# Interleaved columns in a two-layer FFN: ScalarE and VectorE write the activations in token order, instead of TensorE weaving them a second time

## The chip, the cores and the metric

The kernel runs on one core of a Trainium2 chip. The metric is the time of one execution on the device, in microseconds, as the median of several runs. The profile shows one further execution, in which every instruction's start and length were recorded.

## What is computed

The input x holds 4 sequences of 12480 tokens with 128 channels. An attention through 32 learned vectors mixes each sequence, and a feed-forward layer follows:

```python
def mab(q, kv):
    s = scale * (q @ kv.transpose(0, 2, 1))
    s = s - s.max(-1, keepdims=True)
    a = np.exp(s)
    a /= a.sum(-1, keepdims=True) + 1e-09
    return a @ kv
h = mab(I, x)                    # 32 x 128 per sequence
attn = mab(x, h)                 # 12480 x 128 per sequence
h = attn @ w_in                  # 49920 x 2048
g = np.maximum(0.01 * h, h)
return (g @ w_out).astype(np.float32)
```

## The kernel before

The leaky rectifier is split in two: max(0.01 h, h) = 0.01 h + 0.99 max(h, 0). The part with 0.01 is linear, so it needs one product per tile (the linear product, with the matrix m2s). The other part is the feed-forward layer proper. Since attn is a product of attention weights with the 32 x 128 matrix h, the first layer multiplies the attention weights of a tile by h @ w_in, which is prepared once per sequence (hws).

All products of the feed-forward layer use a 32-bit type that TensorE rounds to fewer bits. To keep the precision, values stand as a rounded part and a rest: A4 holds both parts of a tile's attention weights, ghi and glo those of the activations, w_hi and w_lo those of w_out.

The tokens are worked in tiles of 512 (96 of them, and two smaller pair tiles of 384 that take the ends of two sequences). For each tile there are 16 steps, one per block of 128 of the 2048 hidden units; 98 x 16 = 1568 steps in all. A step u is:

- ffn_first: TensorE multiplies A4 by a block of hws into the PSUM tile ph (L821; 3 buffers). ScalarE writes ghi = Relu(ph), rounded (L829). VectorE writes glo = max(ph, 0) - ghi (L831).
- ffn_second: TensorE adds three products to the PSUM tile po of the tile: ghi by w_hi, glo by w_hi, ghi by w_lo (L849). At the last step of a tile the linear product of A4 and m2s is added (L855), and the tile goes to a store: VectorE transposes po in blocks of 32 x 32 into osb (L865), and four DMAs on the SP queue write it to the output (L883).

The order of all instructions is written out in one loop over u: ffn_first of step u + 3, then ffn_second of step u, then one piece each of the work for the coming tiles and the next sequence (first_scores, first_values, second, stack and so on), with a counter, debt, that spaces the pieces that load VectorE.

**Weaving.** A full tile's columns are its 512 tokens in an order that the loads set; call it the tile's order. woven(x, t) is a view that reads or writes the columns of a tile in the order 0, 256, 1, 257, 2, 258 and so on: two streams, 256 floats (1 KB) apart, taken in turn. TensorE reads A4 through it, so the columns of ph, and then of ghi and glo, stand in woven order. It reads ghi and glo through it again, so the columns of po are woven twice. The linear product must match them, so it reads A4 woven twice, as four streams of 128 columns: 0, 128, 256, 384, 1 and so on. The store's DMAs undo this in the rows that they write. Pair tiles are not woven.

Of the kernel before, what the change touches and what calls it, by code (L numbers as in the profile page):

```python
# [9 lines left out]
F32 = mybir.dt.float32  # L10
# [3 lines left out]
AF = mybir.ActivationFunctionType  # L14
# [5 lines left out]
def induced_attention_then_leaky_ffn(  # L20
# [20 lines left out]
    nc = tc.nc  # L41
# [57 lines left out]
    def gen_ps(name):  # L99
        return ps_h.tile([P, TOK], F32, tag="ph", name=name)  # L100
# [14 lines left out]
    xT, xr, ex, aT, A4, hw, maxima, sums_of = {}, {}, {}, {}, {}, {}, {}, {}  # L115
# [668 lines left out]
    tiles = []  # L784
# [8 lines left out]
    def spans(t):  # L793

        got, at = [], 0
        for b, g, js in tiles[t]:
            n = len(js) * 32 * GROUPS[g][2]
            got.append((b, at, n))
            at += n
        return got, at  # L800

    def woven(tile_, t, times=1):

        if len(tiles[t]) > 1:
            return tile_
        if times == 2:
            return tile_.rearrange("p (a b n) -> p n a b", a=2, b=2)
        return tile_.rearrange("p (a n) -> p n a", a=2)

    live, accs = {}, {}  # L810
    slots = [
# [4 lines left out]
    def ffn_first(u):  # L816
        t, f = slots[u]
        parts, n = spans(t)
        ph = gen_ps("ph")
        for b, o, w in parts:  # L820
            nc.tensor.matmul(  # L821
                ph[:, o : o + w],
                hw[b][1][:, f * P : (f + 1) * P],
                woven(A4[t][:, o : o + w], t),
                start=True,
                stop=True,
            )
        ghi = sb.tile([P, TOK], F32R, tag="ghi", name="ghi", bufs=LOOK + 2)
        nc.scalar.activation(ghi[:, :n], ph[:, :n], AF.Relu)  # L829
        glo = sb.tile([P, TOK], F32R, tag="glo", name="glo", bufs=LOOK + 2)  # L830
        nc.vector.scalar_tensor_tensor(  # L831
            out=glo[:, :n],
            in0=ph[:, :n],
            scalar=0.0,
            in1=ghi[:, :n].bitcast(F32),
            op0=ALU.max,
            op1=ALU.subtract,
        )
        live[u] = (ghi, glo)

    def ffn_second(u):
        t, f = slots[u]
        parts, n = spans(t)
        ghi, glo = live.pop(u)
        if f == 0:
            accs[t] = ps_o.tile([P, TOK], F32, tag="po", name="po")
        po = accs[t]
        for w, r in ((w_hi, ghi), (w_hi, glo), (w_lo, ghi)):
            nc.tensor.matmul(  # L849
                po[:, :n], w[:, f, :], woven(r[:, :n], t), start=(f == 0 and r is ghi and w is w_hi), stop=False  # L850
            )
        if f == NF - 1:
            a4 = A4.pop(t)
            for b, o, w in parts:
                nc.tensor.matmul(  # L855
                    po[:, o : o + w], hw[b][2], woven(a4[:, o : o + w], t, 2),
                    start=False, stop=(o + w == n),
                )

    def store(t):  # L860
        _, n = spans(t)
        po = accs.pop(t)
        yield
        osb = sb.tile([P, TOK], F32, tag="osb", name="osb", bufs=3)
        nc.vector.transpose(osb[:, :n], po[:, :n])  # L865
        yield HEAVY
        o = 0
        for b, g, js in tiles[t]:
            base, J, K = GROUPS[g]
            n = 32 * K  # L870
            for j in js:
                row = b * N + base + j * 32 * K
                if len(tiles[t]) > 1:
                    dst = out[row : row + n, :].rearrange("(r k) c -> r k c", k=K)
                else:
                    dst = out[row : row + n, :].rearrange("(v r u) c -> r u v c", v=4, u=K // 4)
                for cb in range(NB):
                    src = osb[32 * cb : 32 * cb + 32, o : o + n]
                    if len(tiles[t]) > 1:
                        src = src.rearrange("p (k c) -> p k c", c=32)  # L880
                    else:
                        src = src.rearrange("p (u v c) -> p u v c", v=4, c=32)
                    nc.sync.dma_start(dst[..., 32 * cb : 32 * cb + 32], src)  # L883
                o += n
            yield
# [39 lines left out]
    with tc.manual_schedule():  # L925
# [9 lines left out]
        for lane in (  # L935
            one, weights, two, one, weights, one, two, weights, one, one, one, two,
        ):
            step(lane)
        ffn_first(0)
        ffn_first(1)  # L940
        step(two)
        step(two)
        step(turning)
        ffn_first(2)
        step(two)
        stacks[0] = stacks[0][QUICK:]
# [6 lines left out]
        for u in range(NT * NF):  # L953
            t, f = slots[u]
            if f == 0 and tiles[t][0][1:] == (0, [0]):
                b = tiles[t][0][0]
# [3 lines left out]
            if u + LOOK < NT * NF:  # L960
                ffn_first(u + LOOK)
            ffn_second(u)
            if f == NF - 1:
                stores.append(store(t))
# [57 lines left out]
```

## Time and profile before

| | |
|---|---|
| median of 3 runs | 1544.82 us (1544.58 to 1544.96) |
| profiled execution | 1544.46 us |
| its span, first to last instruction | 1542.5 us |
| TensorE (PE) busy | 1516.9 us, 98% |
| VectorE (DVE) busy | 1275.1 us, 83% |
| ScalarE (ACT) busy | 1005.4 us, 65% |
| mean granted TensorE clock | 0.992 |

The profile gives for each engine the time in which it had an instruction under way. PE is TensorE's matmuls, PEld its weight loads, which overlap with them. Matmuls overlap each other too, and the recorded length of one contains its passage through the array: matmuls of 380 ns start 216 ns apart. In the rows quoted, L821 is a line of the kernel; "glo<-ph,ghi" names what is written and read; then come partitions x elements; "x1536" counts the instructions; "busy us, mean ns" follow, then the idle time of the engine just ahead of them and what ended it. A row of waits reads: who waited for whom, microseconds in total, how often, longest. SPq is the DMA queue of SP.

### The profile page before, as it was taken

To read this page: it belongs to the slowest core of one execution; us is meant where nothing else is said; L and a number is where in the kernel's file an instruction comes from. 1 tells how busy PE (TensorE), PEld (TensorE's weight loads), DVE (VectorE), ACT (ScalarE), POOL (GpSimd) and SP (SyncE) were. 2 spreads that over 40 slices of the span, in tenths; PEclk is the share of its full clock that TensorE was granted. 3 is DMA by queue.
4 is the path that set the end of the run, shared out by engine and by line. 5 is a ranking of instruction groups with operands and counts; after the bars stand their busy time and mean duration, and the time that the engine had idled before them with its cause. 6 is when DMAs were issued, how large, how long until landed. Compare 5 with 4: busy or idle time off the path is not lost.

```text
span 1542.5 us, 22596 instructions
## 1 busy us (share of the span) xinstructions
PE 1516.9 (98%) x7965; PEld 1271.0 (82%) x7965; DVE 1275.1 (83%) x2245; ACT 1005.4 (65%) x1770; POOL 99.0 (6%) x100
## 2 busy tenths in 40 slices
PE   7799999999999999999999999999999999999998
PEld 5578888888888888888888888888888898888887
DVE  6678889888888888887888888887888888888886
ACT  6356666666666666666666666666666666666665
POOL 2110010000101000000011000000111000000000
PEclk9799999999999999999999999999999999999999
DMA  8133323452243254541314246432302112112211
GB/s 276 17 78 62 69 44 80 98 110 63 60 89 61 36 97 100 99 93 29 72 41 91 49 77 132 95 74 50 76 16 52 24 37 49 35 35 41 43 27 21
DMA packets 401313, 104.21 MB, mean 68 GB/s; under 512 B 372368, under 2 KB 374832, under 8 KB 401200
## 3 DMA queue, kind: packets, MB, share of 16 engines
q1 hardware_dynamic: 401152, 102.75, 32.3%
q8 instruction: 63, 1.03, 0.3%
q14 instruction: 50, 0.41, 0.1%
q10 hardware_dynamic: 48, 0.02, 0.0%
HBM read 48.94 MB, written 25.56 MB: 48 GB/s over the span
## 4 chain that ended last, share of the span: by engine, by line
PE 96%; DVE 2%; ACT 1%; DMA 0%; issue 0%; SPq 0%; DVEq 0%
PE po L849 65%; PE ph L821 23%; PE s_ps L305 3%; PE po L855 2%; PE h_ps L425 1%; DMA xr<-in_x_dram 0%; DVE glo L831 0%; PE xT_ps L538 0%; DVE cv_a L136 0%; ACT ghi L829 0%; PE a_ps L770 0%; ACT xT L544 0%; DVE cv_t L144 0%; PE q_ps L745 0%; DVE ay L453 0%
## 5 line engine op out<-in xcount | busy, mean ns | idle before, releaser
L829 ACT ACTIVATE ghi<-ph 128x512 fp32r<-128x512 f32 (+1 forms) x1568 | 929.4, 595 | 497.2 <-PE ph L821 492.9
L831 DVE SCALAR_TENSOR_TENSOR glo<-ph,ghi 128x512 fp32r<-128x512 f32 (+1 forms) x1568 | 1034.4, 678 | 234.9 <-ACT ghi L829 210.4
L821 PE MATMUL ph<-A,hws 128*128 128x512 f32 (+1 forms) x1600 | 607.6, 383 | 5.1 <-DVE hws L603 2.8
L849 PE MATMUL po<-ghi,w_hi 128*128 128x512 f32 (+1 forms) x1568 | 595.4, 380 | 2.1 <-DVE osb L865 2.1
L849 PE MATMUL po<-glo,w_hi 128*128 128x512 f32 (+1 forms) x1568 | 594.3, 379 | 0.0
L849 PE MATMUL po<-ghi,w_lo 128*128 128x512 f32 (+1 forms) x1568 | 594.3, 379 | 0.0
L821 PEld LDWEIGHTS ph<-A,hws 128*128 128x128 f32 x1600 | 302.7, 190 | 75.3 <-DVE glo L831 21.5
L849 PEld LDWEIGHTS po<-ghi,w_hi 128*128 128x128 f32 x1568 | 297.6, 190 | 46.1 <-issue 3.3
L849 PEld LDWEIGHTS po<-glo,w_hi 128*128 128x128 f32 x1568 | 297.3, 190 | 41.0
L849 PEld LDWEIGHTS po<-ghi,w_lo 128*128 128x128 f32 x1568 | 297.1, 190 | 41.1
L720 POOL TENSOR_TENSOR alo<-aT,ahi 128x512 fp32r<-128x512 f32 x24 | 30.7, 1278 | 683.6 <-ACT ahi L715 681.1
L865 DVE STREAM_TRANSPOSE osb<-po 128x512 f32<-128x512 f32 (+1 forms) x98 | 68.9, 703 | 1.5 <-PE po L855 1.5
L675 POOL TENSOR_TENSOR y<-y,mx 128x512 f32<-128x512 f32 (+1 forms) x27 | 25.3, 937 | 413.8 <-DVE mx L673 413.8
L406 DVE STREAM_TRANSPOSE xT<-xc 128x512 f32<-128x512 f32 x72 | 50.4, 700 | 0.0
L855 PE MATMUL po<-A,m2s 128*128 128x512 f32 (+1 forms) x100 | 43.2, 436 | 0.0
L689 POOL TENSOR_TENSOR y<-y,sm 128x512 f32<-128x512 f32 (+1 forms) x27 | 25.3, 937 | 183.3 <-DVE sm L687 144.7
L425 PEld LDWEIGHTS h_ps<-xr,ay 128*32 128x32 f32 (+1 forms) x784 | 22.0, 110 | 14.3 <-issue 14.3
L425 PE MATMUL h_ps<-xr,ay 128*32 128x128 f32 (+1 forms) x784 | 27.5, 274 | 1.8 <-DVE ay L453 1.8
L305 PE MATMUL s_ps<-xT,indT 128*32 128x512 f32 x192 | 26.3, 621 | 1.3 <-ACT xT L544 1.3
L305 PE MATMUL s_ps<-xT,hT 128*32 128x512 f32 x192 | 25.6, 605 | 0.0
L317 DVE TENSOR_SCALAR_CACHE_REDUCE e<-s_ps 128x512 f32<-128x512 f32 (+1 forms) x28 | 17.1, 610 | 8.7 <-PE s_ps L305 8.5
L855 PEld LDWEIGHTS po<-A,m2s 128*128 128x128 f32 x100 | 18.9, 189 | 2.5
(111 smaller groups left out, 399.3 us busy)
## 6 DMA issues: line engine op xcount, KB each, us to landing
xr<-in_x_dram SPq DMA_DIRECT2D x96, 256.0 KB, 4.5
out_dram<-osb SPq DMA_DIRECT2D x384, 64.0 KB, 2.2
xc<-in_x_dram SPq DMA_DIRECT2D x288, 64.0 KB, 2.7
A<-ahi SPq DMA_DIRECT2D x188, 64.0 KB, 2.0
A<-alo SPq DMA_DIRECT2D x188, 64.0 KB, 2.0
raw<-in_moe_w_in_dram SPq DMA_DIRECT2D x4, 512.0 KB, 6.7
raw<-in_moe_w_out_dram SPq DMA_DIRECT2D x4, 512.0 KB, 7.4
hws<-hwhi SPq DMA_DIRECT2D x24, 64.0 KB, 2.0
```

What stands on the lines that cost most here:

```text
L305: nc.tensor.matmul(dst, lhsT, rhs, start=True, stop=True)
L406: nc.vector.transpose(t[:, j, :], blk.rearrange("p n c -> p (n c)"))
L425: nc.tensor.matmul(hp[32 * k : 32 * k + 32, :C], ay[:rows, 4 * q + k, :], xb[:rows, k, :], start=(q == 0), stop=(4 * q + 4 >= K), tile_pos ...
L675: eng.tensor_tensor(out=yv, in0=yv, in1=mx[:rows, :K].unsqueeze(2).broadcast_to([rows, K, M]), op=ALU.subtract,)
L689: eng.tensor_tensor(out=yv, in0=yv, in1=smv.unsqueeze(2).broadcast_to([rows, K, M]), op=ALU.mult)
L720: (eng or nc.gpsimd).tensor_tensor(out=alo[sl], in0=aT.pop((b, g))[: 32 * J, :], in1=ahi[sl].bitcast(F32), op=ALU.subtract,)
L821: nc.tensor.matmul(ph[:, o : o + w], hw[b][1][:, f * P : (f + 1) * P], woven(A4[t][:, o : o + w], t), start=True, stop=True,)
L829: nc.scalar.activation(ghi[:, :n], ph[:, :n], AF.Relu)
L831: nc.vector.scalar_tensor_tensor(out=glo[:, :n], in0=ph[:, :n], scalar=0.0, in1=ghi[:, :n].bitcast(F32), op0=ALU.max, op1=ALU.subtract,)
L849: nc.tensor.matmul(po[:, :n], w[:, f, :], woven(r[:, :n], t), start=(f == 0 and r is ghi and w is w_hi), stop=False)
L855: nc.tensor.matmul(po[:, o : o + w], hw[b][2], woven(a4[:, o : o + w], t, 2), start=False, stop=(o + w == n),)
L865: nc.vector.transpose(osb[:, :n], po[:, :n])
```

## The change

ScalarE now writes ghi through woven, and reads ph in pairs of neighbours (paired: the same order as before, split in 256 x 2). So column 0 of ph goes to column 0 of ghi, column 1 to column 256, column 2 to column 1: ghi is back in the tile's order. VectorE does the same with glo, and reads ghi, its second input, through woven. The three products of L849 read ghi and glo through woven, as before, and so po is now woven once. The linear product therefore reads A4 woven once, like L821, and each store writes its rows in two halves of 256 instead of four quarters of 128.

```diff
-    def woven(tile_, t, times=1):
+    def woven(tile_, t):
         if len(tiles[t]) > 1:
             return tile_
-        if times == 2:
-            return tile_.rearrange("p (a b n) -> p n a b", a=2, b=2)
         return tile_.rearrange("p (a n) -> p n a", a=2)
+
+    def paired(tile_, t):
+        if len(tiles[t]) > 1:
+            return tile_
+        return tile_.rearrange("p (n a) -> p n a", a=2)
...
-        nc.scalar.activation(ghi[:, :n], ph[:, :n], AF.Relu)
+        nc.scalar.activation(woven(ghi[:, :n], t), paired(ph[:, :n], t), AF.Relu)
...
         nc.vector.scalar_tensor_tensor(
-            out=glo[:, :n],
-            in0=ph[:, :n],
+            out=woven(glo[:, :n], t),
+            in0=paired(ph[:, :n], t),
             scalar=0.0,
-            in1=ghi[:, :n].bitcast(F32),
+            in1=woven(ghi[:, :n].bitcast(F32), t),
...
                 nc.tensor.matmul(
-                    po[:, o : o + w], hw[b][2], woven(a4[:, o : o + w], t, 2),
+                    po[:, o : o + w], hw[b][2], woven(a4[:, o : o + w], t),
...
-                    dst = out[row : row + n, :].rearrange("(v r u) c -> r u v c", v=4, u=K // 4)
+                    dst = out[row : row + n, :].rearrange("(v r u) c -> r u v c", v=2, u=K // 2)
...
-                        src = src.rearrange("p (u v c) -> p u v c", v=4, c=32)
+                        src = src.rearrange("p (u v c) -> p u v c", v=2, c=32)
```

No instruction changes its place on any engine, and none is added or taken away. What changes is the shape of the evacuations and of the stores. The lines below the views move down by four, so L821, L829, L831, L849, L855 and L865 become L825, L833, L835, L853, L859 and L869. On VectorE, in the middle of the program (xT is the transposed input of the next sequence, e its scores), before:

```order
330 L865 STREAM_TRANSPOSE osb<-po 128x512
331 L831 SCALAR_TENSOR_TENSOR glo<-ph,ghi 128x512 x3
332 L406 STREAM_TRANSPOSE xT<-xc 128x512
333 L831 SCALAR_TENSOR_TENSOR glo<-ph,ghi 128x512 x3
334 L406 STREAM_TRANSPOSE xT<-xc 128x512
```

The same place after the change:

```order
330 L869 STREAM_TRANSPOSE osb<-po 128x512
331 L835 SCALAR_TENSOR_TENSOR glo<-ph,ghi 128x256x2 x3
332 L406 STREAM_TRANSPOSE xT<-xc 128x512
333 L835 SCALAR_TENSOR_TENSOR glo<-ph,ghi 128x256x2 x3
334 L406 STREAM_TRANSPOSE xT<-xc 128x512
```

Nothing moved: between two transposes VectorE still has three evacuations, whose 512 elements are now 256 pairs.

## The prediction

> **What bounds the kernel now.** I read the page first: the shares of the engines and the chain that ended last.
>
> ```profile
> span 1542.5 us, 22596 instructions
> PE 1516.9 (98%) x7965; PEld 1271.0 (82%) x7965; DVE 1275.1 (83%) x2245; ACT 1005.4 (65%) x1770; POOL 99.0 (6%) x100
> PE 96%; DVE 2%; ACT 1%; DMA 0%; issue 0%; SPq 0%; DVEq 0%
> ```
>
> The chain is TensorE from end to end: 96% of the span. VectorE is off the chain, but busy 83% of the time, so it is the engine with the least room. Next, the waits and a few stretches of 20 to 100 us (columns: length, then busy time of PE, PEld, DVE, ACT and POOL with counts, granted clock, DMA).
>
> ```profile
> ACT ghi L829 <- PE ph L821: 492.9, 1431, 3.2
> DVE glo L831 <- ACT ghi L829: 210.4, 593, 2.5
> PEld ph L821 <- DVE glo L831: 21.5, 48, 0.8
> ...
> 0.00:60.00 60.00, 46.08 (x475) 33.79 (x476) 37.16 (x120) 31.02 (x67) 11.59 (x14) 0.86 0.60 188
> 60.00:80.00 20.00, 16.52 (x80) 12.74 (x79) 13.53 (x21) 9.32 (x19) 3.79 (x3) 0.91 0.05 7
> 460.00:560.00 100.00, 100.00 (x507) 84.44 (x506) 87.54 (x162) 66.93 (x120) 9.86 (x9) 1.00 0.31 58
> 1360.00:1460.00 100.00, 100.00 (x463) 87.24 (x462) 81.47 (x121) 68.69 (x116) 2.56 (x2) 1.00 0.17 32
> ```
>
> ScalarE waits for TensorE, VectorE for ScalarE, and TensorE for VectorE in only 48 places, 21.5 us in all. From about 80 us on TensorE is never idle, with VectorE 81 to 88% busy beside it. So a nanosecond saved on TensorE in that stretch is a nanosecond of the span, and VectorE can be slowed until its own work fills the span, not further.
>
> **The linear product.** Here are the matmuls by shape and three in a row at a tile's end (start, length).
>
> ```profile
> L821 PE MATMUL ph<-A,hws 128*128 128x512 f32 x1536 | 596.0, 388 | 5.1 <-DVE hws L603 2.8 <-DVE A L778 2.3
> L849 PE MATMUL po<-ghi,w_hi 128*128 128x512 f32 x1536 | 584.0, 380 | 2.1 <-DVE osb L865 2.1
> L855 PE MATMUL po<-A,m2s 128*128 128x512 f32 x96 | 42.5, 443 | 0.0
> ...
> 305.00 0.44 PE L855 MATMUL po<-A,m2s 128*128 128x512 f32 x1
> 305.27 0.38 PE L821 MATMUL ph<-A,hws 128*128 128x512 f32 x1
> 305.49 0.38 PE L849 MATMUL po<-ghi,w_hi 128*128 128x512 f32 x1
> ```
>
> L821 reads A4 woven once (two column streams, 1 KB apart), L849 reads ghi and glo in the same way, L855 reads A4 woven twice (four streams). The first two take 388 and 380 ns, the third 443. The next matmul starts 0.27 us behind L855 and 0.22 us behind L821. After the change L855 reads exactly as L821 does, so it loses 55 to 63 ns; I take 60. On 96 tiles that is 5.8 us (5.3 to 6.0), all on the chain. The three products of L849 keep their reading pattern and gain nothing. The four pair tiles (32 of 1568 steps) are untouched.
>
> **The two evacuations.** Each of 1536 ScalarE instructions now writes ghi in alternation to two halves 1 KB apart, and each of 1536 VectorE instructions reads ghi and writes glo that way. Reading ph in pairs is still reading it in order: nothing.
>
> ```profile
> L829 ACT ACTIVATE ghi<-ph 128x512 fp32r<-128x512 f32 x1536 | 913.7, 597 | 488.0 <-PE ph L821 483.7
> L831 DVE SCALAR_TENSOR_TENSOR glo<-ph,ghi 128x512 fp32r<-128x512 f32 x1536 | 1017.8, 681 | 232.2 <-ACT ghi L829 207.7
> L831 DVE SCALAR_TENSOR_TENSOR glo<-ph,ghi 128x384 fp32r<-128x384 f32 x32 | 16.8, 543 | 2.8 <-ACT ghi L829 2.6
> ...
> L158 DVE TENSOR_REDUCE e<-ident 128x32 f32<-128x128 f32 x1 | 0.4, 369 | 1.3 <-POOL ident masks.py:199 1.3
> L163 DVE TENSOR_REDUCE own<-ident 128x4 f32<-128x128 f32 x1 | 0.3, 278 | 0.0
> L673 DVE TENSOR_REDUCE mx<-y 128x16 f32<-128x512 f32 x24 | 16.2, 675 | 0.0
> ```
>
> Contiguous, VectorE needs (681 - 543) / 128 = 1.08 ns an element at L831. No row of the trace shows a write that jumps at every element. The nearest is a VectorE read that does: L158 reduces 128 elements of the identity with 128 bytes between neighbours, L163 the same 128 in order. They take 369 and 278 ns, 0.71 ns an element apart; L673 and L163 give 1.03 ns an element for reading in order. So one jumping stream costs VectorE 0.71 x 512 = 364 ns per instruction, if two alternating halves are to it what those four streams were. Bounds: 0 (the engine keeps up with two open streams, as TensorE's read of L849 suggests; a gain would be worth nothing, since VectorE is off the chain) and 728 (input and output each pay in full, one behind the other). I take 364: the row is of the same engine, and since the two streams run side by side in one instruction, the slower sets its pace.
>
> The Trainium skill prices this very write: "Vector Engine (DVE) Microarchitecture Reference", section "Measured stream behaviour on trn2 (trn3 not measured)", has 1.71 ns per column where only the destination jumps 4 KiB at each element, 1.98 where all three operands do, against 1.054 in order. Its 1.73 for one jumping source agrees with L158: 278 less 128 x 1.03 leaves 146 fixed, and (369 - 146) / 128 is 1.74. By its figures an instruction would grow by 336 or 474 ns (estimates), and the sum below would come to 1782 or 1994 us.
>
> What VectorE must do in all, if it becomes the bound:
>
> ```profile
> 306.32 0.69 DVE L831 SCALAR_TENSOR_TENSOR glo<-ph,ghi 128x512 fp32r<-128x512 f32 x1 [0.45 <-ACT ghi L829]
> 306.93 0.70 DVE L865 STREAM_TRANSPOSE osb<-po 128x512 f32<-128x512 f32 x1
> ...
> 1534.41 0.69 DVE L831 SCALAR_TENSOR_TENSOR glo<-ph,ghi 128x512 fp32r<-128x512 f32 x1 [0.17 <-ACT ghi L829]
> ...
> 1536.64 0.72 DVE L865 STREAM_TRANSPOSE osb<-po 128x512 f32<-128x512 f32 x1 [1.54 <-PE po L855]
> 1537.39 2.61 SPq L883 DMA_DIRECT2D out_dram<-osb  x4
> ```
>
> An instruction that stands right behind L831 starts 0.61 us after it, though L831 lasts 0.69: 0.08 us of it is a tail that overlaps. Of the 1568, 593 waited for ghi and stood alone; in a full queue each gives back its tail, so VectorE's 1275.1 us shrink to 1275.1 - 593 x 0.08 = 1228. The longer instructions add 1536 x 0.364 = 559: 1787 us. Where VectorE idles whatever its speed: before the first tiles 60 - 37.2 = 22.8, then 20 - 13.5 = 6.5 up to 80 us, and at the end from 1535.1 to 1542.5 less the transpose, 6.7: 36 us. Together 1823 us of span. The profiled execution took 1544.46 us, 2.0 more than its span, and lies 0.4 under the median of 1544.82. **Forecast: 1825 us**, 18% slower. The 5.8 us of L855 are then worth nothing, since TensorE waits: its product of glo stands still until VectorE has written it, and behind that stand the product with w_lo and the next step's first product, so the next Relu, which has time.
>
> VectorE decides from the price at which its sum reaches the shortened TensorE time of 1538.7: (1538.7 - 2 - 36 - 1228) / 1536 = 0.177 us per instruction, 0.35 ns an element. Half of L158's price is enough.
>
> ScalarE: at the same 364 ns it would be busy 1005.4 + 559 = 1564 us, still below VectorE's 1787; queued behind a Relu are only the next Relus and, in the whole program, 1770 - 1568 = 202 other instructions. Bounds 0 and 597 (twice as long). With VectorE unhurt it could bear (1538.7 - 38 - 1005.4) / 1536 = 0.32 us before its busy time fills the span. It sets the end only where its price is at least that and VectorE's is small, and I find no reason for that.
>
> The ring of three ph buffers: matmul 0.38, Relu 0.60 and L831 0.69 become 0.38 + 0.96 + 1.05 = 2.4 us, against three steps of 1825 / 1568 = 1.16 us. Covered by 1.1 us; without that cover the ring would add what it lacks per three steps. The other VectorE work (transposes, reductions, running maxima) keeps its place in the queue and is in the 1228.
>
> **The stores.**
>
> ```profile
> out_dram<-osb SPq DMA_DIRECT2D x384, 64.0 KB, 2.2
> ```
>
> Number, size and the pieces of 32 floats stay; only the rows that one partition owns change (eight neighbours in two halves, not four in four). Four of them take SP 2.61 us and 2.2 to land, once per tile of 14 us, behind three osb buffers: even twice as long they would be hidden, except the last four, which end the program. Cost 0, bounds -1 to +2 us. No queue changes its order: SP and POOL are passed by nothing.
>
> **Rivals.**
> - **Alternating between two halves is free.** TensorE shows it: its two-stream reads (380) run at the pace of the chain, its four-stream read (443) does not, and L158 has four streams. Then only the 5.8 us remain: 1544.5 - 5.8 = 1538.7, faster by 0.4%. Against it: TensorE's reads and VectorE's writes are different paths, and the row of the same engine is L158. The same section of the Trainium skill speaks for it in one remark, that a one-source operation whose read alternates between two regions at each element ran at the full rate. By that, ghi's read is free, but it says nothing of a write.
> - **A price below 0.177 us.** VectorE stays under the span, but with 87.54 of 100 us busy before, it falls behind where first_scores or second add transposes and reductions, and TensorE waits there: 1539 to 1560.
> - **Both streams pay in full.** 1228 + 1536 x 0.728 + 38 = 2384 us. Against it: they run in one instruction side by side.
> - **TensorE's clock falls.** With VectorE the bound, TensorE works 4 x 0.216 of 1.16 us. The stretches above had 0.86 and 0.91 with gaps in TensorE's work. At half the clock a step would take 1.73 us and the whole 2700. Against it: those gaps were of microseconds (the Relu waited up to 3.2), these of a quarter of one.
>
> **How the numbers follow.** VectorE bound by one jumping stream, 0.64: 1825, itself within 1700 to 2010 (282 to 485 ns per instruction: two open streams may cost a fifth less than L158's four, or the second operand may add a third of the price to the first). Free alternation, 0.25: 1538.7. Small price, 0.05, of which faster, the same and slower take 0.01, 0.02 and 0.02. Both in full 0.04, clock 0.02. A measurement of this kernel can tell 0.2% (3 us) from no change. Slower: 0.64 + 0.02 + 0.04 + 0.02 = 0.72; faster 0.26; same 0.02. Free alternation is more than 2 in 10, so the range reaches to it: 1535 to 2010. It leaves out 0.06 above, and about as much from the ends of the two main cases.
>
> **What will show it.** If right: L831 near 1045 ns where it was 681, and near back to back; VectorE over 95% busy from 80 us on; the chain of waits mostly VectorE, glo; TensorE's weight load of L849 waiting for glo, about 0.3 us a step; ScalarE's Relu longer too, with idle time left; L855 near 385 ns. If L831 stays below 0.86 us, the forecast is wrong. If L831 and the Relu are unchanged, the two-stream rival holds, and the gain is L855's alone. Stores landing in much more than 2.2 us, or a granted clock below 0.9 after 120 us, would show a step that I priced at nothing.

## The result, and the profile after

The changed kernel takes 1911.97 us (median of 4 runs, 1908.11 to 1913.09) against 1544.7 us before: a ratio of 1.2376, 95% interval 1.2361 to 1.2391, so 23.8% slower. The forecast was 1825, with a range to 2010. The profiled execution took 1911.1 us. Its page, first the shares of the engines, then the chain that ended last:

```profile
span 1909.0 us, 22496 instructions
PE 1741.8 (91%) x7965; PEld 1170.8 (61%) x7965; DVE 1810.5 (95%) x2245; ACT 1676.1 (88%) x1770; POOL 99.1 (5%) x100
DVE 65%; PE 14%; ACT 12%; issue 5%; SPq 2%; DMA 2%; DVEq 0%; POOL 0%; ACTq 0%
...
out_dram<-osb SPq DMA_DIRECT2D x384, 64.0 KB, 2.2
```

The chain has passed from TensorE (96% before) to VectorE (65%), and VectorE is busy 95% of a longer span. ScalarE, which was at 65%, is at 88% and has 12% of the chain: the forecast gave it none. TensorE's busy time rose from 1516.9 to 1741.8 us with the same 7965 matmuls, so its 91% does not mean that it has more work. The stores land as before. The instructions by shape, and the waits:

```profile
L835 DVE SCALAR_TENSOR_TENSOR glo<-ph,ghi 128x512 fp32r<-128x512 f32 x1536 | 1618.9, 1208 | 65.7 <-ACT ghi L833 64.9
L833 ACT ACTIVATE ghi<-ph 128x512 fp32r<-128x512 f32 x1536 | 1600.8, 1190 | 182.0 <-PE ph L825 180.4
L859 PE MATMUL po<-A,m2s 128*128 128x512 f32 x96 | 36.4, 379 | 0.0
...
PEld ph L825 <- DVE glo L835: 538.6, 1270, 1.9
ACT ghi L833 <- PE ph L825: 190.1, 336, 4.1
PE ph L825 <- DVE glo L835: 134.2, 316, 1.5
DVE glo L835 <- ACT ghi L833: 67.2, 100, 3.3
```

VectorE's evacuation went from 681 to 1208 ns, ScalarE's Relu from 597 to 1190, the linear product from 443 to 379. TensorE now waits for VectorE 1270 times at its weight load for ph, 538.6 us in all: it cannot start the next first product because VectorE has not yet emptied one of the three ph buffers. That is the place where the slower engine shows.

### The profile page after: what moved, and what is told of

It is laid out like the page before. It is cut to its first block, busy times and chain, and to the rows that moved or that the text cites. A ratio compares the mean times of both kernels' runs of the same rounds, so it can differ in the third digit from the quotient of the medians.

```text
span 1909.0 us, 22496 instructions
## 1 busy us (share of the span) xinstructions
PE 1741.8 (91%) x7965; PEld 1170.8 (61%) x7965; DVE 1810.5 (95%) x2245; ACT 1676.1 (88%) x1770; POOL 99.1 (5%) x100
## 4 chain that ended last, share of the span: by engine, by line
DVE 65%; PE 14%; ACT 12%; issue 5%; SPq 2%; DMA 2%; DVEq 0%; POOL 0%; ACTq 0%
DVE glo L835 55%; ACT ghi L833 10%; PE po L853 5%; PE ph L825 5%; DVE osb L869 3%; PE s_ps L305 2%; DVE xT L406 1%; SPq L291 1%; PE h_ps L425 1%; DMA xr<-in_x_dram 1%; DVE y L670 1%; DVE e L317 1%; ACT e L357 1%; DVE ay L453 1%; DVE aT L698 1%
## 5 line engine op out<-in xcount | busy, mean ns | idle before, releaser
L833 ACT ACTIVATE ghi<-ph 128x512 fp32r<-128x512 f32 (+1 forms) x1568 | 1616.6, 1175 | 191.7 <-PE ph L825 190.1
L835 DVE SCALAR_TENSOR_TENSOR glo<-ph,ghi 128x512 fp32r<-128x512 f32 (+1 forms) x1568 | 1635.2, 1195 | 68.1 <-ACT ghi L833 67.2
L825 PE MATMUL ph<-A,hws 128*128 128x512 f32 (+1 forms) x1600 | 736.0, 463 | 145.1 <-DVE glo L835 134.2
L825 PEld LDWEIGHTS ph<-A,hws 128*128 128x128 f32 x1600 | 299.2, 187 | 578.8 <-DVE glo L835 538.6
L853 PE MATMUL po<-ghi,w_hi 128*128 128x512 f32 (+1 forms) x1568 | 595.4, 380 | 3.6 <-DVE osb L869 3.6
L853 PE MATMUL po<-glo,w_hi 128*128 128x512 f32 (+1 forms) x1568 | 594.8, 379 | 0.2
L853 PE MATMUL po<-ghi,w_lo 128*128 128x512 f32 (+1 forms) x1568 | 594.3, 379 | 0.0
L853 PEld LDWEIGHTS po<-glo,w_hi 128*128 128x128 f32 x1568 | 297.5, 190 | 41.9 <-DVE glo L835 1.0
L853 PEld LDWEIGHTS po<-ghi,w_lo 128*128 128x128 f32 x1568 | 297.5, 190 | 40.9
L853 PEld LDWEIGHTS po<-ghi,w_hi 128*128 128x128 f32 x1568 | 297.9, 190 | 8.0 <-issue 4.4
L869 DVE STREAM_TRANSPOSE osb<-po 128x512 f32<-128x512 f32 (+1 forms) x98 | 74.6, 761 | 1.0 <-PE po L859 1.0
L406 DVE STREAM_TRANSPOSE xT<-xc 128x512 f32<-128x512 f32 x72 | 60.4, 838 | 0.0
L859 PE MATMUL po<-A,m2s 128*128 128x512 f32 (+1 forms) x100 | 37.1, 375 | 0.0
L357 ACT ACTIVATE e<-e,nm 128x512 f32<-128x512 f32 (+1 forms) x28 | 19.0, 679 | 5.3 <-DVE zg L356 5.3
```

The costliest lines, as they stand in the source:

```text
L357: nc.scalar.activation(e[:rows, :w], e[:rows, :w], AF.Exp, bias=nm[:rows], scale=SCALE, accum_out=zg[:rows],)
L406: nc.vector.transpose(t[:, j, :], blk.rearrange("p n c -> p (n c)"))
L825: nc.tensor.matmul(ph[:, o : o + w], hw[b][1][:, f * P : (f + 1) * P], woven(A4[t][:, o : o + w], t), start=True, stop=True,)
L833: nc.scalar.activation(woven(ghi[:, :n], t), paired(ph[:, :n], t), AF.Relu)
L835: nc.vector.scalar_tensor_tensor(out=woven(glo[:, :n], t), in0=paired(ph[:, :n], t), scalar=0.0, in1=woven(ghi[:, :n].bitcast(F32), t), op ...
L853: nc.tensor.matmul(po[:, :n], w[:, f, :], woven(r[:, :n], t), start=(f == 0 and r is ghi and w is w_hi), stop=False)
```

## The experiments

There are three jumping operands: ScalarE's output, VectorE's second input and VectorE's output. Any of them can be put in order by itself (by views of another order; the values are then not the reference's, as the expectations say). Lengths of instructions are means over 1536 of them. A recorded length includes a tail that the next instruction overlaps, and the tail differs between the runs; where that matters, the time from the start of one evacuation to the start of the next is given beside it, as a mean over those that follow each other without idle time (about 380 pairs in the kernel before, over 1000 in the others named). linear_once and read_side were run five times, every other variant once. The kernel before, run beside them, took 1543.56 to 1544.58 us in single runs, and 1544.02 as the median of nine beside linear_once and read_side.

**ScalarE's output alone** (act_out):

```diff
-            out=woven(glo[:, :n], t),
+            out=paired(glo[:, :n], t),
...
-            in1=woven(ghi[:, :n].bitcast(F32), t),
+            in1=paired(ghi[:, :n].bitcast(F32), t),
```

> Only ScalarE jumps: it writes ghi to two halves in turn; VectorE reads ghi and writes glo in order (the values of glo and the output's rows are then not the reference's). Theory 'own': each engine pays for its own jumping stream, whatever the other does. Then the Relu takes about 1190 ns as in the changed kernel, VectorE's evacuation 681 as before, and ScalarE, with 1005 + 1536 x 0.59 = 1911 us less its overlapping tails, sets the end near 1650 us. Theory 'shared': part of the price comes from both engines jumping at once. Then the Relu takes its shortest length there, about 1040 to 1080, and the time is 1545 to 1600 us.

Measured: 1644.82 us. By shape:

```profile
L833 ACT ACTIVATE ghi<-ph 128x512 fp32r<-128x512 f32 x1536 | 1454.8, 1157 | 63.9 <-PE ph L825 63.5
L835 DVE SCALAR_TENSOR_TENSOR glo<-ph,ghi 128x512 fp32r<-128x512 f32 x1536 | 1038.7, 684 | 311.5 <-ACT ghi L833 304.1
```

The Relu's length grows by 560 ns with VectorE entirely in order: 1157 ns lies near the 1190 of theory "own" and above the 1040 to 1080 of "shared". ScalarE is busy for 93% of the span and has 52% of the chain, TensorE 37%. ScalarE alone would have made the change 6.5% slower.

**VectorE's output alone, input alone, and both** (dve_out, dve_in, dve_both; each with the plain Relu of before):

```diff
-        nc.scalar.activation(woven(ghi[:, :n], t), paired(ph[:, :n], t), AF.Relu)
+        nc.scalar.activation(ghi[:, :n], ph[:, :n], AF.Relu)
...
-            in1=woven(ghi[:, :n].bitcast(F32), t),     # dve_out; out= likewise in dve_in; neither in dve_both
+            in1=paired(ghi[:, :n].bitcast(F32), t),
```

> Only VectorE's output jumps; ScalarE writes in order and VectorE reads ghi in order (glo's values and the output's rows are not the reference's). By the forecast's step (one jumping stream costs 364 ns) L835 takes 1045 ns and the time is 1820 us. If the output is free and the input pays: 681 ns and 1539 us. If the price needs both streams of the instruction: under 900 ns.

> Only VectorE's second input jumps: it reads ghi from two halves in turn and writes glo in order; ScalarE writes in order (values not the reference's). If a read from two alternating halves pays like the four-stream read of L158: 1045 ns, 1820 us. If two alternating streams are free to read, as for TensorE: 681 ns, and 1539 us, the gain of the linear product alone.

> VectorE reads and writes with jumps, as in the changed kernel; ScalarE writes ghi in order (values not the reference's). Theory 'own': L835 stays at about 1200 ns and the time near 1900 us. Theory 'shared': without the jumping ScalarE it falls to 1026 to 1050 ns, and the time to about 1810 to 1830 us, the forecast. If the two streams of the instruction add in part: 1100 to 1150 ns and 1850 to 1900 us.

Measured: 1760.41, 1539.32 and 1820.3 us. L835 by shape, first in the run with the output:

```profile
L835 DVE SCALAR_TENSOR_TENSOR glo<-ph,ghi 128x512 fp32r<-128x512 f32 x1536 | 1467.9, 1069 | 37.2 <-ACT ghi L833 36.5
```

with the input:

```profile
L835 DVE SCALAR_TENSOR_TENSOR glo<-ph,ghi 128x512 fp32r<-128x512 f32 x1536 | 1027.3, 688 | 215.6 <-ACT ghi L833 197.8
```

with both (and the page's shares of that run):

```profile
L835 DVE SCALAR_TENSOR_TENSOR glo<-ph,ghi 128x512 fp32r<-128x512 f32 x1536 | 1538.7, 1123 | 30.7 <-ACT ghi L833 30.5
...
PE 1679.3 (92%) x7965; PEld 1175.3 (65%) x7965; DVE 1752.9 (96%) x2245; ACT 1007.9 (55%) x1770; POOL 99.2 (5%) x100
```

Reading from two halves in turn is nearly free: 688 against 681 ns. Writing so adds 388 ns to the length. Reading and writing so in one instruction adds 442, so the read adds 54 where the write jumps too. With VectorE alone jumping the kernel takes 1820 us. The expectations hold in part. dve_out has about the length that was expected (1069 ns for 1045) and ends 60 us earlier than the 1820 expected with it. dve_both has the length of "add in part" (1100 to 1150 ns) and the time of "shared" (1810 to 1830 us). The tail explains both: from start to start L835 takes 587 ns in the kernel before, 910 in dve_out and 954 in dve_both, so the spacing grows by 322 and 367 ns where the lengths grow by 388 and 442.

**Does the number of streams matter?** dve_in4 is dve_in with VectorE's second input read from four quarters instead of two halves:

```diff
-            in1=woven(ghi[:, :n].bitcast(F32), t),
+            in1=woven4(ghi[:, :n].bitcast(F32), t),     # full tiles: "p (a n) -> p n a", a=4; out and in0 in order, plain Relu
```

> As the run in which only VectorE's second input jumps, but between four quarters of ghi (0, 128, 256, 384, 1 and so on) instead of two halves (values not the reference's). The forecast took its price from a read of four streams 128 bytes apart, 0.71 ns an element dearer than one in order. If four streams pay where two did not: L835 at about 1000 to 1050 ns, 1740 to 1825 us. If the number of streams doesn't matter and L158's price came from something else: 688 ns and 1539 us.

Measured: 1830.61 us.

```profile
L847 DVE SCALAR_TENSOR_TENSOR glo<-ph,ghi 128x512 fp32r<-128x512 f32 x1536 | 1512.8, 1046 | 29.9 <-ACT ghi L845 29.5
```

Four streams cost 365 ns (1046 against 681) where two cost 7, and the time lies just above the 1740 to 1825 us expected for that. So L158's 364 ns was a right price for its own pattern, and that pattern was not the change's. The edit also halves the distance between neighbours, from 1024 to 512 bytes; number and distance were not separated, but L158, with four streams 128 bytes apart, has the same price per element (0.71 ns, here 365 / 512 = 0.71). The lengths mislead here: 1046 ns is less than dve_both's 1123, yet the kernel takes 10 us longer. From start to start the two take 958 and 954 ns.

**ScalarE's and VectorE's outputs without the jumping input** (act_dve_out), **and ScalarE's output with VectorE's input** (act_out_dve_in):

```diff
-            in1=woven(ghi[:, :n].bitcast(F32), t),     # act_dve_out
+            in1=paired(ghi[:, :n].bitcast(F32), t),
...
-            out=woven(glo[:, :n], t),                  # act_out_dve_in
+            out=paired(glo[:, :n], t),
```

> The changed kernel, but VectorE reads ghi in order: both engines' outputs jump, no input does (values not the reference's). So far L835 took 1069 ns with the output alone and 1123 with input and output, and 1208 with ScalarE jumping too; the Relu 1157 alone and 1190 with VectorE jumping. If the jumping read adds its 54 ns here as well, L835 takes 1150 to 1160 ns, and the time is about 1850 us. If the jumping read only counts where writes collide less: 1190 to 1210 ns, and about 1900 us.

> The eighth combination: ScalarE's output and VectorE's input jump, VectorE's output is in order (values not the reference's). If the reads of two halves stay free as long as VectorE itself writes in order: Relu 1157 ns, L835 688, 1645 us, as with ScalarE's output alone. If those reads get in the way of any jumping write at a distance of 1024 bytes, as the run with 1056 suggests: the Relu over 1200 ns, L835 over 740, and over 1700 us.

Measured: 1806.22 and 1645.47 us. The first:

```profile
L835 DVE SCALAR_TENSOR_TENSOR glo<-ph,ghi 128x512 fp32r<-128x512 f32 x1536 | 1476.7, 1065 | 74.3 <-ACT ghi L833 73.4
L833 ACT ACTIVATE ghi<-ph 128x512 fp32r<-128x512 f32 x1536 | 1490.4, 1097 | 183.6 <-PE ph L825 182.1
```

and the second:

```profile
L835 DVE SCALAR_TENSOR_TENSOR glo<-ph,ghi 128x512 fp32r<-128x512 f32 x1536 | 1046.1, 692 | 304.0 <-ACT ghi L833 297.6 <-ACT y L681 0.2
L833 ACT ACTIVATE ghi<-ph 128x512 fp32r<-128x512 f32 x1536 | 1455.3, 1160 | 63.7 <-PE ph L825 63.0
```

Two engines that write with jumps hardly slow each other's instructions: L835 takes 910 ns from start to start alone and 913 beside the jumping Relu, the Relu 923 alone and 928 beside the jumping L835. The kernel still takes 46 us longer than with VectorE's output alone (1806 against 1760): VectorE waits 75.4 us for ghi, where it waited 38.6, and is busy 10 us longer. My two expectations for the first run lay at 1850 and 1900 us, and both were too high. In the second run the jumping read is nearly free beside ScalarE's jumping writes. It is the three together that add: 143 ns to the length of L835 (1208 against 1065) and 93 to the Relu's (1190 against 1097), 106 us of the changed kernel's time. From start to start L835 goes from 913 to 983 ns; 1536 times 70 ns are 108 us.

Instructions that read and write in order become longer as well. VectorE's transpose of the next sequence, before and after the change:

```profile
L406 DVE STREAM_TRANSPOSE xT<-xc 128x512 f32<-128x512 f32 x72 | 50.4, 700 | 0.0
...
L406 DVE STREAM_TRANSPOSE xT<-xc 128x512 f32<-128x512 f32 x72 | 60.4, 838 | 0.0
```

In the runs with one or two jumping operands it takes 681 to 716 ns. That suggests that part of what the three add together lies in something that the engines share, and not in the jumping instructions alone; no run here shows what it is.

**The distance of the halves** (gap):

```diff
-        ghi = sb.tile([P, TOK], F32R, tag="ghi", name="ghi", bufs=LOOK + 2)
+        ghi = sb.tile([P, 2 * 264], F32R, tag="ghi", name="ghi", bufs=LOOK + 2)     # glo likewise; halves at 0 and 264 in every view of the two
```

> The changed kernel with the two halves of ghi and glo 1056 bytes apart instead of 1024, the rest as it is, and the same result. If the writes are slow because both halves meet in one part of the memory at a distance of a power of two: L835 and the Relu fall below 900 ns and the time below 1700 us. If the price is in leaving a place after one element, wherever the next one lies: about 1200 and 1190 ns, 1905 to 1915 us.

Measured: 1807.85 us.

```profile
L843 DVE SCALAR_TENSOR_TENSOR glo<-ph,ghi 128x512 fp32r<-128x512 f32 x1536 | 1482.1, 1075 | 76.5 <-ACT ghi L841 75.5
L841 ACT ACTIVATE ghi<-ph 128x512 fp32r<-128x512 f32 x1536 | 1496.0, 1110 | 180.6 <-PE ph L833 179.6
```

Neither expectation holds. The price of the writes stays, but nearly all that the jumping input added is gone: 1075 and 1110 ns are close to the 1065 and 1097 of the run without it. So 104 us hung on how the tiles lie. The edit changes the distance of the halves (1024 to 1056 bytes) and, with the tiles' size, also the distance between buffers; which of the two counts was not separated.

**Which jumps cost a write** (act_pairs, act_step2; as act_out, with another order of ScalarE's output):

```diff
-        nc.scalar.activation(woven(ghi[:, :n], t), paired(ph[:, :n], t), AF.Relu)
+        nc.scalar.activation(woven_pairs(ghi[:, :n], t), quads(ph[:, :n], t), AF.Relu)   # act_pairs: out "p (a n e) -> p n a e", e=2
+        nc.scalar.activation(step2(ghi[:, :n], t), halves(ph[:, :n], t), AF.Relu)        # act_step2: out "p (n a) -> p a n"
```

> As the run in which only ScalarE's output jumps, but it writes two neighbouring elements to each half before it changes (0, 1, 256, 257, 2, 3 and so on; values and the output's order are not the reference's). If each change of place costs a fixed time, half as many cost half: the Relu near 880 ns instead of 1157, and the time near 1545 us. If a run of two neighbours fills what one access to memory takes, pairs are free: 597 to 610 ns and 1539 us. If it is the strided pattern as such: 1157 ns, 1645 us.

> Only ScalarE's output changes place: it writes every second element of ghi, first the even ones and then the odd, so neighbours in time are 8 bytes apart (values and the output's order not the reference's). Alternating halves cost 560 ns per Relu, pairs 47. If each write that does not continue the pair before costs, as single elements do: about 1150 ns, 1645 us. If what counts is the leap to a far place and two writes still fall into one 16-byte piece: 597 to 880 ns, and 1539 to 1545 us.

Measured: 1539.42 and 1556.47 us. The Relu in pairs:

```profile
L845 ACT ACTIVATE ghi<-ph 128x512 fp32r<-128x512 f32 x1536 | 985.5, 644 | 414.1 <-PE ph L837 411.0
```

and with every second element:

```profile
L845 ACT ACTIVATE ghi<-ph 128x512 fp32r<-128x512 f32 x1536 | 1285.8, 861 | 139.1 <-PE ph L837 131.2
```

With two neighbours written before each change of half, half as many changes add 47 ns to the length in order; single elements added 560. So on ScalarE a change of place costs little when a pair of neighbours is complete. A step of 8 bytes, which never completes a pair but stays near, adds 264, about half. Neither expectation has the time of the step-of-two run: it is slower than before by 13 us although ScalarE is busy for only 88% of it. I take that for queueing at the places where ScalarE has other work; its 11% of the chain suggests it, and no run tests it.

**The linear product by itself** (linear_once):

```diff
-                    po[:, o : o + w], hw[b][2], woven(a4[:, o : o + w], t, 2),
+                    po[:, o : o + w], hw[b][2], woven(a4[:, o : o + w], t),
```

> The kernel before with one edit: the linear product reads A4 woven once (its columns then don't match po's, so its share of each row is another token's). By the forecast's step the matmul falls from 443 to 380 or 388 ns and the time by 5.3 to 6.0 us, to 1539. If the four-stream read were hidden anyway: no change.

Measured: 1538.41 us against 1544.02, a ratio of 0.9963 (0.995 to 0.9975).

```profile
L855 PE MATMUL po<-A,m2s 128*128 128x512 f32 x96 | 36.4, 379 | 0.0
```

64 ns less on 96 products is 6.1 us; the medians differ by 5.6.

**The same permutation on the reading side** (read_side). ph is read with every second column, first the even ones, and ghi and glo are written in order:

```diff
-        nc.scalar.activation(woven(ghi[:, :n], t), paired(ph[:, :n], t), AF.Relu)
+        nc.scalar.activation(halves(ghi[:, :n], t), split_(ph[:, :n], t), AF.Relu)
...
+    def split_(tile_, t):                                    # pair tiles pass through both unchanged
+        return tile_.rearrange("p (n a) -> p a n", a=2)
+    def halves(tile_, t):
+        return tile_.rearrange("p (a n) -> p a n", a=2)      # in order; L835 uses both in the same way
```

> The same permutation as in the change, but done by the reads: ScalarE and VectorE read ph with every second element, first the even columns and then the odd, and write ghi and glo in order; everything else is as in the changed kernel, and so is the result. Theory 'jumping writes': the price sits in writing, the read of ph from PSUM at a stride of two costs nothing or little. Then the Relu takes about 597 ns, L835 about 681, and the time is 1539 us, 5 to 6 under the kernel before. Rival 'any stride pays': a stride of two in PSUM costs as VectorE's four-stream read of L158 did, 0.71 ns an element: L835 at 1045 ns, the time near 1800 us.

Measured: 1538.66 us against 1544.02, a ratio of 0.9962 (0.9948 to 0.9975). By shape:

```profile
L841 DVE SCALAR_TENSOR_TENSOR glo<-ph,ghi 128x512 fp32r<-128x512 f32 x1536 | 1017.4, 681 | 226.4 <-ACT ghi L839 202.9
L839 ACT ACTIVATE ghi<-ph 128x512 fp32r<-128x512 f32 x1536 | 913.8, 597 | 482.8 <-PE ph L831 479.0
...
PE 96%; DVE 2%; ACT 1%; DMA 0%; issue 0%; SPq 0%; DVEq 0%
```

Both evacuations have the lengths of before to the nanosecond, TensorE carries the chain again, and the whole gain of the linear product stays (379 ns). This version computes the same as the changed kernel and is faster than it and than the kernel before.

## Why the prediction was right, and where its steps were not

- **TensorE bounds the kernel, VectorE has the least room.** Right: the chain went from TensorE to VectorE once L835 grew.
- **The linear product, 60 ns and 5.8 us.** Right: 64 ns; by itself 5.6 us; in the changed kernel worth nothing.
- **VectorE's 364 ns and 1825 us.** With only VectorE jumping the kernel takes 1820.3 us. That the sum comes so close is in part luck. L158 was a read of four streams, and that price (365 ns on L835) does not apply to two: the input read costs 7 ns, the output 388, both 442. With 442 the forecast's own sum gives 1228 + 1536 x 0.442 + 38 = 1945 us. It misses because it holds the overlapping tail at 0.08 us: the tail was 681 - 587 = 94 ns before and is 1123 - 954 = 169 ns in dve_both. From start to start L835 grew by 954 - 587 = 367 ns, and that this is L158's 364 is chance: the price was right for a write that the row did not show.
- **ScalarE at the same price, below VectorE, nothing added.** This is the step that failed. The Relu grew by 560 ns alone, not 364. Its tail grew too, so that ScalarE is busy for 1532.3 us in act_out, where the forecast had 1564; yet it sets the end at 1645 us, for which I had found no reason. Beside VectorE it adds what the forecast lacks: 1911.1 against 1820.3 in the profiled executions, 91 us. Of that VectorE's busy time has 1810.5 - 1752.9 = 57.6, as all three operands together slow each other, and its waits for ghi 67.2 - 32.7 = 34.5.
- **Bounds 0 and 728.** They held. The step to 527 (681 to 1208) is a write's price plus what three jumping operands add together, which the forecast had as one jumping stream. 527 is above the 485 that the forecast's upper end of 2010 us stands for, and by its sum would be 2075 us; the time stayed inside the range because the tail had grown to 1208 - 983 = 225 ns. With the 983 - 587 = 396 ns from start to start the sum gives 1874 us, and the waits that ScalarE adds bring it near the 1911 measured. L835 near 1045 ns, the first of the signs that I had named, is missed.
- **The rule of the Trainium skill** ("Vector Engine (DVE) Microarchitecture Reference", "Measured stream behaviour on trn2 (trn3 not measured)"): with the destination alone its 1.71 ns, measured there with jumps of 4 KiB, made 336 ns more and 1782 us. dve_out took 1760 us, and L835 was 388 ns longer by its length and 322 from start to start. Its remark that a read alternating between two regions runs at the full rate, which I let speak for the free rival, is true here for the read (688 ns). The rival fell by the write, on which the page's table had the answer.
- **The ring of three ph buffers, and where TensorE waits.** The size was right (about 0.3 us a step: 538.6 us / 1568 = 0.34), the place was not. I had TensorE waiting for glo at the second product; its weight loads waited there 2 times, 1.0 us in all. It waits at the next first product, for the ph buffer that the late evacuation still holds, and so ph's ring is where a slow evacuation is felt.
- **Stores and clock at nothing.** Right: stores land in 2.2 us as before, and the granted clock was 0.992 in both.

## What to carry to other kernels

Put a permutation on the side that reads, if the read is one that costs nothing, and not on the side that writes: here it cost 367 us as writes of single elements to two places in turn (with the read of ghi that goes with them), and nothing as a read of PSUM with every second element. A read of four quarters cost VectorE about as much as the write (365 and 388 ns). If the write must jump, let it finish two neighbours first (47 ns instead of 560 on ScalarE; VectorE was not tried). And a price from the nearest row is only as good as its likeness: two streams and four, reads and writes, VectorE and ScalarE each had another, so both engines of a chain need a price of their own. And take a price from the time between starts, not from recorded lengths: their tails overlap, and here they grew with the price.

## What the hardware showed that I had not expected

- Two alternating streams are nearly free to read and four are not on VectorE (688 and 1046 ns, 681 in order); on TensorE a read of four takes 443 ns where two take 379. Two are already dear to write (1069 on VectorE, 1157 on ScalarE).
- A jumping read that is nearly free by itself adds 54 ns to the length of an instruction whose write jumps, and 143 when ScalarE's writes jump too; then even VectorE's transposes, which are in order, take 838 ns instead of 700. With the halves 1056 bytes apart instead of 1024, in larger tiles, L835 took 1075 ns, 10 more than without the jumping read at 1024 bytes, and the kernel 104 us less.
- Reading PSUM with a step of two elements cost neither ScalarE (597 ns) nor VectorE (681 ns) anything.
